# Two more token tiles turned by DMA, x1 on ScalarE's queue, W1 in four parts, no throwaway matmuls between the first transposes, and a new instruction order

## The chip, the cores and the metric

The kernel runs on one core of a Trainium2 chip. The metric is the device time of one execution in microseconds (us); the kernel before takes 150.0 us, the median of three runs (149.98 to 150.35). A core has five instruction streams that run side by side and meet by semaphores: TensorE (PE, matmuls), VectorE (DVE), ScalarE (ACT), GpSimd (POOL) and SyncE (SP). SP computes nothing here; it issues DMAs. ACT and POOL can issue DMAs too.

## The reference

One input x of 2048 tokens by 640 features, in bf16, is normalised, and two branches of the result are added to x:

```
xn  = (x - mean(x)) / sqrt(var(x) + 1e-5)                 # over the 640 features
A   = irfft2( rfft2(xn) * (w_r + 1j * w_i) )               # over tokens and features, in bf16 out
B   = gelu_tanh( xn @ w1 + b1 ) @ w2 + b2                  # 640 -> 1536 -> 640
out = x + A + B
```

The weights are w_r and w_i (2048 x 321), w1 (640 x 1536), b1, w2 (1536 x 640) and b2.

## The kernel before

**Tiles.** The 2048 tokens are 16 tiles of 128 (tile c holds the tokens 16p + c, p the partition). Per tile, DVE takes statistics in two halves (`bn_stats`, L661) and joins them (`bn_aggr`, L663), POOL raises the variance to the power -0.5 (L665), and DVE normalises (L683). The normalised tile goes two ways.

- For branch B it is needed turned, as xnT (features on partitions). Tiles 0 to 5 are turned on PE: five 128x128 transposes against the identity (L702) into PSUM and a copy out of it by DVE or ACT (L557/L558; for tiles 0 and 1 three blocks by DVE and two by ACT). Tiles 6 to 15 (`BYDMA`) are turned by one DMA transpose each, issued on SP (L690).
- For branch A, DVE folds pairs of tiles (L714, L718), and PE begins the transform with ten matmuls for a pair against a table `gtab` ("aps"). Later stages go by the names bps, cps, the filter on DVE (L819, L823), dps, DMA transposes of U (L844), and eps.

**Branch B.** `BLOCKS` groups the tiles as 0, 1, 2-3, 4-5, 6-7, 8-11, 12-15. For each block and each of 12 column blocks of W1, five matmuls (issued as a step of three and a step of two, "hps") fill a PSUM bank, and ACT applies gelu (L752). A group of block 4-5 can't begin before both its tiles are turned. W1 is loaded in three parts, `W1P`: column blocks 0-2 (480 KB), 3-6 (640 KB) and 7-11 (800 KB); a group waits for the part that holds its columns. The second matmul ("kps" for tiles kept early, "fps" for the others) and the last transform step are summed in PSUM, DVE adds x + b2 (L930) and SP stores the tile (L933).

**Order.** Every operation has a number, in the order in which the program builds them, and `ORDER` lists for each of the five engines the numbers in the order of issue. An engine works strictly down its list and waits where an operand is not ready; nothing is reordered while the kernel runs. So a wait in one stream delays all that stands behind it there. `Sched.schedule()` only uses its planned times to choose PSUM banks and buffers; the lists are fixed.

**The start**, as the lists have it:

- SP: x0, x1, W1 part 0, W1 part 1, x2-3, W1 part 2, gtab, x4-5, x6-7, then m, x14-15, e, a part of W2, and so on.
- ACT: b1, the table load for gelu, the identity, then copies and gelu.
- PE: 38 throwaway matmuls on a zeroed tile (`idle(WARM[0], ...)`), two transposes of tile 0, 6 more throwaway matmuls (`idle(WARM[1], ...)`), the little transpose of b1, three transposes of tile 0, five of tile 1, then the groups of blocks 0 and 1.
- DVE: statistics of tile 0, statistics of tile 1, normalise 0, join 1, normalise 1, the copy of three turned blocks of tile 0.

The calls of L541 are loads by the helper `load`; nearly all matmuls are recorded at the helper's line L546, and all copies at L557 (ACT) and L558 (DVE).

Of the kernel before, what the change touches and what calls it, by code (L numbers as in the profile page):

```python
# [9 lines left out]
ACT = mybir.ActivationFunctionType  # L10
# [114 lines left out]
class Pool:  # L125
# [31 lines left out]


ORDER = {
    "sp": """8 12 13 14 15 16 17 18 19 32 28 31 23 33 46 27 47 24 20 25 37 43 164 166 29 48 177 179 190 192 40 41  # L160
34 49 38 42 205 217 219 203 39 30 26 35 36 45 44 521 522 548 546 545 547 524 523 50 569 570 571 572 51 596 595 593
594 622 613 658 649 639 685 675 694 757 748 766 731 711 782 721 798 791 805""",
    "pe": """7 114 115 52 112 120 118 231 237 238 234 267 232 235 268 270 271 273 274 249 243 244 246 247 285 250 286 276 277 282 283 279
280 240 241 291 292 258 259 297 252 253 261 298 262 134 137 294 128 295 288 129 289 327 321 328 322 324 325 146 145 303 306 309
307 304 333 310 334 149 152 330 318 312 313 331 315 319 316 160 336 337 161 354 363 355 366 367 369 370 364 357 372 358 360 373
339 340 264 361 265 173 342 343 174 378 384 385 387 379 396 397 388 393 405 406 348 394 349 345 375 346 187 186 376 408 351 390
409 352 391 200 199 255 423 441 442 424 414 213 212 438 426 256 415 439 226 227 411 420 486 435 427 412 483 436 450 421 504 451
432 433 501 447 448 429 489 606 430 607 608 525 609 417 418 518 632 456 633 381 528 457 634 382 635 515 642 643 644 495 645 459
492 668 669 539 460 453 542 454 670 552 671 402 549 444 300 301 403 498 445 399 704 400 573 705 678 679 563 680 706 566 707 681
576 714 724 725 726 715 727 716 717 587 741 474 590 480 481 475 742 743 468 744 471 472 616 469 617 465 466 462 463 597 477 478  # L170
623 618 652 653 659 619 620 654 695 611 655 656 688 689 637 732 690 647 691 692 751 683 673 752 760 753 754 767 761 762 729 755
746 763 776 764 709 777 792 778 793 785 779 780 786 719 787 788 789 794 795 796 799 800 801 802 803""",
    "act": """11 9 10 53 116 121 239 233 269 272 236 275 245 248 251 287 278 284 281 242 293 260 299 254 135 296 263 132 130 131 290 326
329 323 147 308 305 311 150 335 153 314 332 320 317 338 162 356 368 371 365 359 341 362 266 374 344 175 386 380 389 398 407 350
347 395 188 410 353 392 201 377 702 425 443 604 214 215 257 440 229 722 416 630 488 413 485 428 422 505 452 437 676 503 434 640
490 431 527 526 712 449 419 519 520 666 529 458 383 516 496 494 541 544 455 461 554 550 404 302 499 446 401 574 686 575 564 567
739 577 578 589 614 592 476 591 482 749 473 650 758 470 467 464 598 479 783 624 660 774 697 696 734 733 769 768""",
    "dve": """0 54 55 56 58 59 111 60 117 113 122 119 123 124 126 63 66 62 65 64 67 125 127 133 136 140 139 138 142 143 144 141
73 69 72 70 74 71 79 77 76 148 151 80 154 78 155 81 158 156 159 157 163 165 93 167 90 168 86 83 84 172 87 171
85 88 94 169 95 170 176 91 178 100 92 180 181 189 191 182 101 184 108 102 185 183 98 193 194 97 195 99 196 198 107 197  # L180
202 104 204 109 105 206 207 106 209 211 208 210 218 216 220 221 222 223 225 224 230 228 487 484 506 502 508 512 507 491 511 509
510 514 513 610 530 531 536 532 535 517 537 533 636 497 534 646 538 493 540 543 553 672 551 556 560 500 559 555 557 558 561 562
565 568 708 682 580 584 579 583 582 585 581 728 586 718 588 745 599 600 601 602 603 625 626 627 629 661 628 621 612 662 657 663
664 665 638 648 699 698 693 701 700 684 674 736 735 737 738 770 771 756 747 765 730 773 772 710 781 720 790 797 804""",
    "pool": """2 3 1 57 61 68 22 75 21 4 6 82 89 5 96 103 110 605 703 723 677 631 667 641 713 740 687 651 750 615 784 759
775""",
}


# [17 lines left out]

ROW_NS = {256: 26, 384: 22, 512: 27, 640: 33, 642: 70, 768: 37, 1024: 47, 1280: 56, 1600: 68, 2560: 103, 4096: 160, 10272: 750, "acc": 152}
TAIL = 0.9
LAG = ((1.6, 1.1), (3.9, 2.8), (16.0, 1.6), (60.0, 0.0))  # L210


LAT = {"pe": 0.2, "dve": 0.125, "act": 0.16, "pool": 0.12}
# [2 lines left out]
class Sched:  # L216
# [38 lines left out]
    def schedule(self):  # L255
# [31 lines left out]
        while left:  # L287
            best = None
            for e in self.engines:
                cands = []  # L290
                for o in [p for p in pend[e] if p is fixed[e][len(self.order[e])]] if fixed and len(self.order[e]) < len(fixed[e]) else pend[e]:
# [17 lines left out]
                    t = max(r, free[e])  # L309
# [11 lines left out]
                t, o = min(near, key=lambda c: (-c[1].prio, c[1].seq))  # L321
# [4 lines left out]
            t, e, o = best  # L326
# [8 lines left out]
            if o.nbytes:  # L335
                n, size = o.rows
                ring = rings[e]
                free[e] = ring.issue_end(t, dur, n)
                turn = size == 256 and n == 40
                done = max(t + ring.lead, free[e] - dur + ring.lead, dma_last if turn else dma_free) + n * ROW_NS[size] / 1e3  # L340
                dma_last = max(dma_last, done + lag(t, size))
                if e == "act":
                    done = t + ring.lead + 0.5
                    dma_free += n * ROW_NS[size] / 1e3
                else:
                    dma_free = done
                ring.held.append((done, n))
                o.end = done + TAIL + lag(t, size)
            else:
                o.end = t + dur + LAT[e]  # L350
            for b in o.writes:
# [92 lines left out]


BLOCKS = [(0, 1), (1, 1), (2, 2), (4, 2), (6, 2), (8, 4), (12, 4)]
W1P = [(0, 3), (3, 7), (7, 12)]
GROUPS = [(0, 2), (2, 3), (5, 3), (8, 3), (11, 3), (14, 2)]
BYDMA = tuple(range(6, 16))
ANY = [(0, 8)]  # L450
ZONE = {"hps": [(4, 8)], "bps": [(0, 4)], "cps": [(0, 4)], "dps": [(0, 4)],
        "eps": [(0, 4)], "fin": [(4, 8), (0, 4)], "fps": [(4, 8)], "tps": ANY, "aps": ANY}
# [7 lines left out]
GP = (-81.0, 42.0, 4.0, 72.0, -32.0, 6.0, -9.0)  # L460
G1 = 1
WAVE = (0, 3, 0, 0, 2, 0, 0, 4, 0, 2, 0, 2, 4, 2, 2, 3)
WARM = (38, 6)


def bass_parallel_sum__spectral_gfnet__dense_activation_gelu__prompt_kernel(
# [21 lines left out]
    with ExitStack() as es:  # L488
# [104 lines left out]
            a, b = W1P[j]  # L593
            load(view(W1, 128 * a, [[F, 5], [1, 128 * (b - a)]]), w1v[:, :, 128 * a:128 * b], B_w1s[j], (40, 256 * (b - a)), q=q)
        load_x(0, 1)
        K.op([("act", 1.3)], 420, lambda e, _: e.preload_act_table(ACT.Gelu_apprx_tanh), writes=[Buf("table")])
        load(ident[:], const["I"], B_id, (8, 256), q="act", prio=410)
        load(b1t[:], b1v, B_b1, (1, 256), q="act", prio=405)
        load_x(1, 1)
        load_w1(0)  # L600
        load_w1(1)
        load_x(2, 2)
        load_w1(2)
        load(gtab[:], const["G"], B_g, (8, 4096), issue=0.5)
        load_x(4, 2)
        load_x(6, 2)
# [45 lines left out]
        norm_ops, ring_ops, a_ops, TD = [], [], [], {}  # L652
        B_rs = [Buf(f"rstd{c}") for c in range(16)]
        mv_ops, st_op = [], {}
        for c0, n in [(0, 1), (1, 1)] + [(c, 2) for c in range(2, 16, 2)]:
            pr = 100 - c0 / 2
            B_mv, B_r = Buf(f"mv{c0}"), Buf(f"r{c0}")
            for c in range(c0, c0 + n):
                B_st = Buf(f"st{c}")
                for h in range(2):  # L660
                    st_op[c] = K.op([("dve", 0.393)], pr, lambda e, _, c=c, h=h: e.bn_stats(stats[:, c, 6 * h:6 * h + 6], view(X, c * D + H2 * h, [[1, H2]])),  # L661
                         reads=[B_x[c]], writes=[B_st], gate=mv_ops[:1])
                mv_ops.append(K.op([("dve", 0.119)], pr, lambda e, _, c=c: e.bn_aggr(mv[:, c, :], stats[:, c, :]), reads=[B_st, B_eps], writes=[B_mv]))  # L663
            a, b = c0, c0 + n
            K.op([("pool", 0.65)], 500, lambda e, _, a=a, b=b: e.tensor_tensor(out=rstd[:, a:b], in0=mv[:, a:b, 1], in1=mhalf[:, a:b], op=ALU.pow),  # L665
                 reads=[B_mv, B_mh], writes=[B_r] + B_rs[a:b])

        for pair in range(8):
# [10 lines left out]
            for n in range(2):  # L679
# [16 lines left out]
                for j0, j1, engs in ((0, 3, ["dve"]), (3, 5, ["act"])) if c < 2 else ((0, 5, ["dve", "act"]),):  # L696
                    nj = j1 - j0
                    tps = Buf(f"tps{c}", psum, 1, ZONE["tps"])

                    def xt(e, _, n=n, xnv=xnv, tps=tps, j0=j0, j1=j1):  # L700
                        for j in range(j0, j1):
                            ins = e.transpose(psb(tps.slot, [[1, 512]]).bitcast(BF)[:, 128 * j:128 * j + 128], xnv(n, 128 * j, [[1, 128]]), ident[:])  # L702
                        return ins
                    tp = K.op([("pe", nj * mm_us(128))], pr, xt, reads=[B_xn, xn, B_id], writes=[tps], alts=[[("128", nj * mm_us(128))]])
                    if j0 and not c:
                        idle(WARM[1], WARM[1] * 0.07, gate=[tp])
                    us = {"dve": 0.06 + 0.07 * nj, "act": act_us(128 * nj)}
                    o = K.op([(e, us[e]) for e in engs], pr,
                         copy(lambda c=c, j0=j0, j1=j1: xnT[:, c, j0:j1, :],
                              lambda tps=tps, j0=j0, j1=j1: psb(tps.slot, [[1, 512]]).bitcast(BF)[:, 128 * j0:128 * j1].rearrange("p (j t) -> p j t", j=j1 - j0)),  # L710
                         reads=[tps], writes=[B_xnT[c]])
# [261 lines left out]
```

## Time and profile before

| what | value |
|---|---|
| median of three runs | 150.0 us |
| the profiled execution | 149.5 us |
| span in its trace | 147.5 us, so 2.0 us lie around the span |
| PE busy | 142.1 us, 96% of the span |
| DVE, ACT, POOL busy | 106.8, 87.4, 22.4 us |
| granted PE clock | 1.00 over the span |
| DMA | 23.35 MB, mean 158 GB/s |
| first group of branch B starts on PE | 7.20 us |
| last matmul's chain piece ends | 145.07 us |

Times inside the trace count from the start of the span. A row of the chain of waits gives start, duration, and the work on which the end depends; in a merged row of the timeline, "x38" is the number of instructions, and the idle time before the first, if any, stands in brackets with what ended it. Matmuls are pipelined, so a duration of one (219 ns for a 128-column one) is longer than the distance to the next.

### The profile page before, as it was taken

What the parts mean: (1) busy time and instruction counts of PE and PEld (TensorE: products, weight loads), DVE (VectorE), ACT (ScalarE), POOL (GpSimd) and SP (SyncE); (2) the same over time, 40 slices, a digit from 0 to 9 for tenths busy, and PEclk for the clock granted to TensorE, in tenths of its full rate; (3) what the DMA queues carried; (4) which work ended last, traced back from release to release, by engine and by line L of the source; (5) the groups of instructions that cost most, each with busy time, mean ns of one, the idle gap of its engine ahead of it and who ended that gap; (6) DMA issues with size and microseconds to landing.
All of it is one profiled execution on the core that took longest, in us unless ns stands there. A gap on an engine that the chain in (4) does not pass through costs nothing.

```text
span 147.5 us, 4184 instructions
## 1 busy us (share of the span) xinstructions
PE 142.1 (96%) x1753; PEld 93.0 (63%) x1772; DVE 106.8 (72%) x227; ACT 87.4 (59%) x164; POOL 22.4 (15%) x37
## 2 busy tenths in 40 slices
PE   7999999999999999999999999999999999999993
PEld 7799999988555355456545554554456666556572
DVE  2798999999943469369957966882206969899872
ACT  3288999788998985962547774306587354403000
POOL 1301520401100029040000003000044420000000
PEclk9999999999999999999999999999999999999999
DMA  4999999899989907946406695992639947023233
GB/s 119 325 392 385 349 222 125 212 125 185 157 151 284 200 14 177 260 85 155 43 0 60 126 101 142 146 187 79 132 58 221 212 92 221 21 84 122 107 129 127
DMA packets 30890, 23.35 MB, mean 158 GB/s; under 512 B 19224, under 2 KB 27544, under 8 KB 30744
## 3 DMA queue, kind: packets, MB, share of 16 engines
q1 hardware_dynamic: 28336, 17.48, 51.7%
q0 software_dynamic: 2368, 5.57, 17.5%
q8 instruction: 14, 0.23, 0.7%
q10 hardware_dynamic: 168, 0.04, 0.1%
q14 instruction: 4, 0.03, 0.1%
HBM read 13.58 MB, written 2.62 MB: 110 GB/s over the span
## 4 chain that ended last, share of the span: by engine, by line
PE 93%; DVE 2%; issue 2%; DMA 2%
PE ps L546 92%; DMA X<-in_A_x_dram 2%; PE ps L702 1%; DVE stats L661 1%; DVE T L683 0%; DVE xnT L558 0%; DVE W L930 0%; DVE mv L663 0%
## 5 line engine op out<-in xcount | busy, mean ns | idle before, releaser
L546 PE MATMUL ps<-xnT,W 128*128 128x256 bf16 (+2 forms) x420 | 59.0, 288 | 0.2
L546 PE MATMUL ps<-W,gT 128*128 128x128 bf16 (+3 forms) x378 | 55.7, 291 | 1.6 <-issue 0.9
L546 PEld LDWEIGHTS ps<-W,gT 128*128 128x128 bf16 x396 | 30.0, 98 | 24.0 <-issue 2.2
L546 PEld LDWEIGHTS ps<-xnT,W 128*128 128x128 bf16 x420 | 34.3, 98 | 15.4 <-issue 1.7
L752 ACT ACTIVATE gT<-ps,b1col 128x256 bf16<-128x256 f32 (+2 forms) x84 | 38.4, 512 | 8.7 <-PE ps L546 8.0
L661 DVE BATCH_NORM_STATS2 stats<-X 128x6 f32<-128x320 bf16 x32 | 14.2, 476 | 2.4 <-DMA X<-in_A_x_dram 2.4
L557 ACT ACTIVATE Wf<-ps 128x960 bf16<-128x960 f32 (+1 forms) x9 | 7.6, 879 | 13.3 <-PE ps L546 13.3
L915 POOL DMA_DIRECT2D X<-in_A_x_dram x8 | 7.2, 1350 | 44.5 <-DMA XV<-gtab 23.6
L819 DVE TENSOR_TENSOR T<-Y,Wf 128x1288 bf16<-128x1288 bf16 x16 | 12.4, 824 | 1.3 <-DMA Wf<-in_A_w_i_dram 0.9
L915 POOL DMA_DIRECT2D xnT<-in_A_x_dram x8 | 7.1, 1182 | 24.1 <-DMA XV<-gtab 16.3
L557 ACT ACTIVATE U<-ps 128x512 bf16<-128x512 f32 (+1 forms) x12 | 4.6, 439 | 9.7 <-PE ps L546 9.7
L665 POOL TENSOR_TENSOR rstd<-mv,mhalf 128x2 f32<-128x2 f32 (+1 forms) x9 | 6.3, 698 | 25.5 <-DVE mv L663 25.5
L557 ACT ACTIVATE Xb<-ps 128x960 bf16<-128x960 f32 (+1 forms) x6 | 6.8, 1141 | 5.2 <-PE ps L546 5.0
L557 ACT ACTIVATE Y<-ps 128x644 bf16<-128x644 f32 x11 | 7.6, 708 | 3.8 <-PE ps L546 3.7
L557 ACT ACTIVATE XV<-ps 128x1280 bf16<-128x1280 f32 (+3 forms) x11 | 9.5, 895 | 0.0
L558 DVE CAST Y<-ps 128x644 bf16<-128x644 f32 x5 | 4.1, 828 | 7.0 <-PE ps L546 7.0
L558 DVE CAST Xb<-ps 128x960 bf16<-128x960 f32 (+1 forms) x6 | 6.7, 1122 | 3.0 <-PE ps L546 3.0
L718 DVE TENSOR_TENSOR T<-T 128x512 bf16<-128x512 bf16 (+1 forms) x32 | 8.5, 308 | 0.1
L930 DVE TENSOR_TENSOR W<-ps,xnT 128x640 bf16<-128x640 f32 (+2 forms) x10 | 6.7, 686 | 1.9 <-PE ps L546 1.9
L930 DVE TENSOR_TENSOR W<-ps,X 128x640 bf16<-128x640 f32 x8 | 6.5, 817 | 2.0 <-PE ps L546 1.8
L683 DVE TENSOR_SCALAR T<-X,mv,rstd 128x640 bf16<-128x640 bf16 x16 | 6.6, 440 | 1.5 <-POOL rstd L665 1.5
L546 PE MATMUL ps<-getab,XV 32*128 32x160 bf16 (+1 forms) x128 | 7.6, 242 | 0.0
(50 smaller groups left out, 135.9 us busy)
## 6 DMA issues: line engine op xcount, KB each, us to landing
X<-in_A_x_dram POOLq DMA_DIRECT2D x8, 320.0 KB, 4.8
xnT<-in_A_x_dram POOLq DMA_DIRECT2D x8, 320.0 KB, 5.0
W<-in_B_w_dram SPq DMA_DIRECT2D x5, 480.0 KB, 5.5
out_dram<-W SPq DMA_DIRECT2D x15, 160.0 KB, 1.8
X<-in_A_x_dram SPq DMA_DIRECT2D x7, 320.0 KB, 9.9
Wf<-in_A_w_i_dram SPq DMA_DIRECT2D x6, 160.5 KB, 7.3
Wf<-in_A_w_r_dram SPq DMA_DIRECT2D x6, 160.5 KB, 4.8
W<-in_B_w_dram SPq DMA_DIRECT2D x1, 800.0 KB, 8.1
```

The costliest lines, as they stand in the source:

```text
L546: ins = e.matmul(o_, lhsT=lw, rhs=rh, start=st, stop=sp_, skip_group_check=True)
L557: return e.activation(dst(), src(), ACT.Copy, scale=scale)
L558: return e.tensor_copy(dst(), src())
L661: st_op[c] = K.op([("dve", 0.393)], pr, lambda e, _, c=c, h=h: e.bn_stats(stats[:, c, 6 * h:6 * h + 6], view(X, c * D + H2 * h, [[1, H2]]) ...
L665: K.op([("pool", 0.65)], 500, lambda e, _, a=a, b=b: e.tensor_tensor(out=rstd[:, a:b], in0=mv[:, a:b, 1], in1=mhalf[:, a:b], op=ALU.pow), ...
L683: o = K.op([("dve", 0.356)], pr, lambda e, _, c=c, n=n, xnv=xnv: e.tensor_scalar(out=xnv(n, 0, [[1, D]]), in0=view(X, c * D, [[1, D]]), sc ...
L702: ins = e.transpose(psb(tps.slot, [[1, 512]]).bitcast(BF)[:, 128 * j:128 * j + 128], xnv(n, 128 * j, [[1, 128]]), ident[:])
L718: ring_ops.append(K.op([("dve", dve_us(4 * w, 2))], pr, lambda e, _, op=op, x1v=x1v, xfv=xfv, o_=o_, o0=o0, o1=o1, w=w: e.tensor_tensor(ou ...
L752: K.op([("act", act_us(128 * nt, 1))], pr + PRIO["gelu"] + GP[bi], lambda e, _, c0=c0, nt=nt, fc=fc, hps=hps: e.activation(gT[:, fc, 128 * ...
L819: filt_ops.append(K.op([("dve", dve_us(4 * KP, 2))], pr, lambda e, _, k=k, Y=Y, TB=TB, pair=pair: e.tensor_tensor(out=view(TT, TB.slot * 8 ...
L915: xo_ops[c] = K.op([("pool", 0.9)], 51 - c / 20, lambda e, _, c=c, xov=xov: e.dma_start(xov(0, D), xv[:, c, :], accum_op=ALU.add), reads=[ ...
L930: K.op([("dve", dve_us(w))], 95, lambda e, _, os_=os_, fps=fps, o0=o0, w=w, xov=xov, base=base: e.tensor_tensor(out=view(W1, OST + os_.slo ...
```

## The change

- `BYDMA` begins at 4: tiles 4 and 5 are turned by DMA transposes on SP. Their ten PE transposes and their two copies out of PSUM (both on ACT before) go.
- x1 is loaded through ACT's queue, behind b1 and ahead of the identity; the table load comes after the three. On SP, W1 part 0 is the second load.
- W1 comes in four parts: 480, 640, 480 (column blocks 7-9) and 320 KB (10-11). SP's list is now x0, W1 part 0, W1 part 1, x2-3, W1 part 2, gtab, x4-5, x6-7, W1 part 3, x8-9, b2, a part of W2, the transposes of tiles 4 and 5, x10-11, two loads of w_i, the transposes of tiles 6 and 7, and so on.
- The 6 throwaway matmuls go (`WARM = (38, 0)`). PE's list begins: 38 throwaway matmuls, b1's transpose, tile 0's five transposes, tile 1's five, groups.
- The powers of tiles 2 and 3 are taken one by one on POOL.
- All five lists are new. DVE now joins tile 1's statistics before it normalises tile 0. Of the copies out of PSUM some have passed from ACT to DVE and the other way: tile 3's turned copy and some of Y, U, Xb to ACT, two of the "aps" copies and some of Y, U, Xb to DVE.
- In the planner, two numbers that place the planned landing of DMAs change; they reach the kernel only through the choice of banks.

```diff
 ORDER = {
-    "sp": """8 12 13 14 15 16 17 18 19 32 28 31 23 33 46 27 47 24 20 25 37 43 164 166 29 48 177 179 190 192 40 41
+    "sp": """8 13 14 15 16 18 19 20 17 21 28 30 150 152 25 44 48 163 165 26 29 42 178 176 191 189 27 32 46 31 41 38
...
-    "pe": """7 114 115 52 112 120 118 231 237 238 234 267 232 235 268 270 271 273 274 249 243 244 246 247 285 250 286 276 277 282 283 279
+    "pe": """7 53 116 114 119 121 230 233 234 236 231 237 272 273 269 270 266 267 275 276 278 239 279 284 240 281 285 282 245 246 242 243
...
-    "act": """11 9 10 53 116 121 239 233 269 272 236 275 245 248 251 287 278 284 281 242 293 260 299 254 135 296 263 132 130 131 290 326
+    "act": """9 10 11 12 54 117 122 235 232 238 274 271 268 277 280 241 286 283 247 244 289 256 259 136 139 253 292 131 325 295 132 304
...
-LAG = ((1.6, 1.1), (3.9, 2.8), (16.0, 1.6), (60.0, 0.0))
+LAG = ((1.1, 1.1), (3.9, 2.8), (16.0, 1.6), (60.0, 0.0))
...
-                dma_last = max(dma_last, done + lag(t, size))
+                late = 0.0 if e == "act" else lag(t, size)
+                dma_last = max(dma_last, done + late)
...
-                o.end = done + TAIL + lag(t, size)
+                o.end = done + TAIL + late
...
-W1P = [(0, 3), (3, 7), (7, 12)]
+W1P = [(0, 3), (3, 7), (7, 10), (10, 12)]
-BYDMA = tuple(range(6, 16))
+BYDMA = tuple(range(4, 16))
-WARM = (38, 6)
+WARM = (38, 0)
...
         load_x(0, 1)
-        K.op([("act", 1.3)], 420, lambda e, _: e.preload_act_table(ACT.Gelu_apprx_tanh), writes=[Buf("table")])
+        load(b1t[:], b1v, B_b1, (1, 256), q="act", prio=425, issue=0.65)
+        load_x(1, 1, q="act")
         load(ident[:], const["I"], B_id, (8, 256), q="act", prio=410)
-        load(b1t[:], b1v, B_b1, (1, 256), q="act", prio=405)
-        load_x(1, 1)
+        K.op([("act", 1.3)], 405, lambda e, _: e.preload_act_table(ACT.Gelu_apprx_tanh), writes=[Buf("table")])
         load_w1(0)
         load_w1(1)
         load_x(2, 2)
         load_w1(2)
+        load_w1(3)
...
-        for c0, n in [(0, 1), (1, 1)] + [(c, 2) for c in range(2, 16, 2)]:
+        for c0, n in [(c, 1) for c in range(4)] + [(c, 2) for c in range(4, 16, 2)]:
...
-                    if j0 and not c:
-                        idle(WARM[1], WARM[1] * 0.07, gate=[tp])
```

In the new lists 8, 10, 15, 19, 20 and 21 are the loads of x0, x1, x2-3, x4-5, x6-7 and x8-9; 13, 14, 16 and 17 the parts of W1; 18 is gtab; 150 and 152 are the DMA transposes of tiles 4 and 5, 163 and 165 those of 6 and 7; 53 is b1's transpose on PE.

## The prediction

> **What bounds the kernel now.** I read the page first: the span, PE's row of busy slices, and the summary of the chain that ended last.
>
> ```profile
> span 147.5 us, 4184 instructions
> ...
> PE   7999999999999999999999999999999999999993
> ...
> PE 93%; DVE 2%; issue 2%; DMA 2%
> ```
>
> PE is full from the second slice to the last and is 93% of the chain. So an edit is worth what it takes from PE's work, or what it moves PE's first useful matmul, and a late operand costs in full: no idle time exists in which it could hide. Next the chain in order of time, for the start.
>
> ```profile
> 0.74 2.29 DMA X<-in_A_x_dram
> ...
> 3.98 0.22 DVE mv L663
> 4.20 0.74 DVE stats L661 x2
> 4.94 0.41 DVE T L683
> 5.35 0.05 issue
> 5.40 0.40 PE ps L702 x2
> 5.79 0.68 PE ps L546 x7
> 6.47 0.29 PE ps L702 x3
> ...
> 6.78 0.37 DVE xnT L558
> 7.15 0.05 issue
> 7.20 4.33 PE ps L546 x70
> 11.53 0.10 issue
> ...
> 19.24 0.56 PE ps L702 x10
> ```
>
> Useful work starts at 7.20. Ahead of it lie x0's load, DVE, two transposes, 0.68 us of throwaway matmuls with b1's transpose, three more transposes and a copy. The last row is tiles 4 and 5 on PE. Then a table by stage, who issued the existing DMA transposes and how long they took.
>
> ```profile
> 0.00:7.20 7.20, 5.95 (x56) 5.30 (x56) 3.36 (x11) 1.96 (x4) 1.55 (x9) 1.00 0.73 218
> 7.20:13.00 5.80, 5.70 (x95) 5.31 (x96) 4.84 (x16) 4.78 (x17) 0.70 (x1) 1.00 1.06 393
> 13.00:22.00 9.00, 9.00 (x113) 8.34 (x111) 8.98 (x30) 8.81 (x21) 2.95 (x6) 1.00 1.07 305
> 22.50:36.30 13.80, 13.80 (x148) 12.59 (x147) 13.62 (x46) 12.10 (x27) 2.26 (x4) 1.00 1.03 160
> ```
>
> ```profile
> L690 SPq DMA_TRANSPOSE xnT<-T x10: 1201/1280/2519, 21.7 to 41.7; - x10
> ...
> DMA to landing us min/median/max: 2.6/3.9/5.0
> ```
>
> Columns of the table: stretch, its length, busy PE, weight load, DVE, ACT, POOL, granted clock, DMA share, GB/s. DMA is full from 7.2 on, DVE from 13, ACT is at 88% in the last stretch.
>
> **The change, part by part.** The sum is made in the profiled execution: span 147.5, own time 149.5, so 2.0 around it; the median of the runs is 150.0, 0.5 higher, and I add that at the end.
>
> *Tiles 4 and 5 off PE.* Ten transposes leave the chain: -0.56 (row 19.24). Their copies leave ACT (0.75 and 0.77 in the timeline), which PE did not wait for: 0. Bounds: -0.72 (their busy time) to -0.50.
>
> *The two transposes on SP.* SP must wait for DVE's normalised tiles, and x10, loads of w_i, and tiles 6 and 7 queue behind. In DVE's new list, between normalise 3 (ended 12.83 before, 12.2 to 12.8 now) and normalise 4 stand two folds (0.90), four halves of statistics (1.67), two joins (0.34) and three small folds (0.9): normalise 4 is done at 16.4 to 17.0, normalise 5 one us later. SP needs 1.28 per transpose, so the second is issued at about 17.9. The queue ahead of them is 4672 KB, 4.78 MB. The table moves 1.57 MB by 7.2, 2.28 by 13.0, and the rest at 305 GB/s by about 16.1, so they find little ahead of them. Landing 2.6 to 5.0 later: 20.5 to 22.9; with the median 21.8. PE began block 4-5 at 22.92 before. Ahead of it now stand one more group for tile 0 and one for tile 1 (0.56), ten transposes less (0.56), so it moves with the start alone, to 22.5. Cost 0, bounds 0 to 0.4 by the transposes' own rows; loads issued at 11.7 to 12.8 took 9.9 to 11.7, and by that far row the wait would be 6. I take 0 as the queue is empty by then. Tiles 6 and 7 are wanted about one us earlier than before (at 27.7; landed then by 26.9): 0.
>
> *The start.* Normalise 0 now stands behind tile 1's join, and a join holds DVE 0.14 to 0.22: normalise 0 ends at 5.5. Then b1's transpose is already done, and five transposes follow with nothing between; at the distance of the throwaways (38 in 4.24 us, so 0.106 each) they end by 6.3. Tile 1's join comes 0.31 earlier, so does its power on POOL (0.56), and normalise 1 leaves DVE free at 6.2. The copy (0.37) ends at 6.7 and the first group starts at 6.75 instead of 7.20: -0.45. Bounds: +0.2 (the join alone counts, if something else holds the copy) and -0.6.
>
> *x1 on ACT's queue.* ACT issues it behind b1 (0.62), at about 1.4. DVE wants it at 4.1. The nearest rows: x0 and x1 landed 2.3 and 2.4 after issue, the identity on ACT's own queue 2.3 after 1.42. So 3.8: cost 0. Far row: the 480 KB part took 4.7, which would be 6.1 and delay the whole start by 2.0. The table load (1.28) now ends near 3.6, b1's column is wanted at 7: 0.
>
> *W1 behind x0, four parts.* Part 1 landed at 8.4, and PE wants it after six groups (1.7) at 8.45: 0. Part 2 landed at 11.5 (3.41 + 8.1); 320 KB less at 393 GB/s is 0.8 sooner, and SP is 0.46 earlier without x1: 10.2 to 10.7 against a need at 10.4. gtab (3.88 + 8.9) likewise 11.5 to 12.0 against 11.8. Tile 2 must be normalised by 11.5; with its own join and power it takes some 0.6 less than the 2.75 between x2's landing (2.71 + 6.6) and 12.03, so 11.4 to 11.9. Together 0 to 0.8; I take 0.2, and the 0.1 at 11.53 goes: +0.1.
>
> The Trainium skill (Trainium Kernel Development and Optimization, Key Constraints) says that SP's, ACT's and POOL's DMAs share the same 16 engines, so that a second issuer only saves issue time. By it x1's bytes still stand beside W1's, the later ends hold, and this item would be about 0.5 rather than 0.1; no row here shows x1 there.
>
> *The new order elsewhere.* Same matmuls in another sequence: 0. Final steps end on the same three pieces of tile 15, last store 1.6 after issue: 0. Bounds in the rivals.
>
> Sum: -0.56 - 0.45 + 0.1 = -0.9. Span 146.6, own time 148.6; on the median's scale **149.1**.
>
> **Rivals.** *ScalarE full.* From 22.5 to 36 ACT's new list holds 21 gelus (0.42, the 23 rows' 9.7 us), one small one (0.4), two copies of 1.24 and four copies of b2 (0.75) that stood behind 38 before: 14.7 us, against 13.8 of PE. Back to back five gelus took 1.84, 0.37 each, which makes 13.5. DVE, 13.62 of 13.80, gets one of ACT's copies as well. So PE waits for banks or folds 0 to 0.9; with the upper end 149.9, no change. For: both sums are near 100%. Against: ACT idled 1.7 there and PE never waited.
>
> *PE's clock stays slow.* The timeline has 38 throwaways at 0.106 from 0.99; the 128-column groups from 7.20 run at 95 in 5.99, 0.063. The speed changes inside the six throwaways that go, after some 5.2 us of nearly unbroken work. If the longer break (5.1 to 5.6, then two short ones) starts that stretch anew, it ends at 10.8, and the 4.0 us from 6.75 are done at half speed: 2.0, less the 0.3 that loads would make PE wait anyway. 150.8, slower. It decides from the point at which the change of speed comes later than about 8.5. Against: before, 0.4 without a matmul did not prevent it, and transposes also fill the stretch (eight at 6.40 took 0.71).
>
> The Trainium skill (TensorE: Matmul & The Clock Gate, Part 1 and Part 4) has a free-running window of 3.4 us after which a busy array is released, and says that transposes don't engage the full clock. By it a missed window ends 3.4 later and costs 1.4: 150.5. The trace agrees that both speeds exist, and shows transposes at the fast one; whether they count as work it can't show.
>
> *Turned tiles late.* Landing at 23.8 instead of 21.8 (the slowest row, 5.0, and 0.9 more if the queue ahead isn't empty) stops PE at block 4-5 for 1.3: 150.4. For: PE has no slack. Against: the transpose issued at 24.26, with an empty queue, took 2.6. It decides from 22.5 on.
>
> *x1 late.* From 4.1 on each us is a us; with the far row 151.1.
>
> **Chances.** Forecast 0.50 (148.6 to 149.6 by the bounds of the start and the loads), ScalarE full 0.16, turned tiles late 0.13, clock 0.10, x1 late 0.06, another wait of over one us from the new lists 0.05. About 0.3%, 0.45 us, can be told from no change: faster below 149.55. The forecast gives 0.50 and a mild case of ScalarE 0.04 to faster; the rest of ScalarE, and half a us of lateness in the tiles, 0.18 to the same; slower 0.28. The range runs from the best ends of the bounds (-0.72, -0.6, -0.1: 148.6, less 0.1 for scatter) to the slow clock; the far ends are left out: 148.5 to 150.8.
>
> **What would show it.** Right: in the chain, ten transposes at 19 gone, the first 70-matmul piece at 6.7 to 6.8, PE busy without a gap at 22.5, last piece ending near 144.2. Wrong: normalise 0 waiting for x1; 128-column matmuls 0.106 apart after 6.8; PE idle before the first 256-column group of block 4-5 with a DMA of L690 as releaser; ACT without idle time from 22 to 36 and PE's weight loads released by gelu.

## The result and the profile after

The changed kernel took 151.66 us (median; 150.70 to 152.40) against 149.99 us: a ratio of 1.0123 (95% interval 1.0083 to 1.0163). Forecast were 149.1 us and a gain; 151.66 lies above the range. The profiled execution took 152.04 us.

The page after, answering to the three lines of before:

```profile
span 150.1 us, 4173 instructions
...
PE   7499999999999999999999999999999999999993
...
PE 93%; DMA 4%; ACTq 1%; DVE 0%; issue 0%
```

PE is full to the end as before. Only the second slice (3.75 to 7.5 us) differs: a 4 where a 9 stood. The chain's DVE share has gone, and 4% of DMA has come. The chain in order of time (start, duration, what) says which DMA:

```profile
1.40 0.37 ACTq L542
...
1.80 5.62 DMA ident<-c_I
7.42 0.05 issue
7.47 0.19 PE ps L547
7.65 1.18 PE ps L704 x10
8.83 6.87 PE ps L547 x83
...
16.59 131.10 PE ps L547 x1561
```

The identity, issued at 1.80 behind x1 on ACT's queue, lands at 7.42; before, it landed at 3.75. b1's transpose stands at the head of PE's list and needs it, so PE idles from 5.2 to 7.47. The first group starts at 8.75 by the timeline (7.20 before, 6.75 forecast). From there nothing stops PE: one piece of 1561 matmuls runs from 16.59 to 147.69, and the row of tiles 4 and 5 at 19.24 is gone. So what was lost was lost ahead of 16.6. The 83 matmuls from 8.83 carry the second loss, which an experiment below sizes.

The identity ended the last wait, but x1 was close behind it. DVE's rows in the timeline:

```profile
5.59 0.89 DVE L663 BATCH_NORM_STATS2 stats<-X 128x6 f32<-128x320 bf16 x2 [1.31 <-DMA X<-in_A_x_dram]
6.65 0.38 DVE L685 TENSOR_SCALAR T<-X,mv,rstd 128x640 bf16<-128x640 bf16 x1
7.49 0.45 DVE L685 TENSOR_SCALAR T<-X,mv,rstd 128x640 bf16<-128x640 bf16 x1 [0.46 <-POOL rstd L667]
```

DVE's new list joins tile 1's statistics before it normalises tile 0, so normalise 0 (6.65) waited for x1 too, although its power was there at 4.94; this is a sign of being wrong that the prediction named. Normalise 1 ended at 7.94, and tile 1's transposes stand ahead of the first group. With the identity on time tile 1's transposes could have begun at 7.99 and the first group, by an estimate, at about 8.5 (in the run below with the identity ahead of x1, at half speed too, it started 0.51 behind the first of them: 9.40 and 9.91). So most of the 2.0 us is x1's, and the identity adds 0.2 to 0.3.

The loads issued in the first 2.2 us (the last number is the time from issue to landing):

```profile
X<-in_A_x_dram SPq DMA_DIRECT2D x1, 160.0 KB, 2.4
X<-in_A_x_dram ACTq DMA_DIRECT2D x1, 160.0 KB, 4.2
ident<-c_I ACTq DMA_DIRECT2D x1, 32.0 KB, 5.6
```

x1 took 4.2 on ACT's queue and landed at 5.57, where the forecast had 3.8. The 32 KB of the identity took longer than the 160 KB of x1.

### The profile page after: what moved, and what is told of

Read it like the earlier page. It is cut to its first block, busy times and chain, and to the rows that moved or that the text cites. A ratio compares the mean times of both kernels' runs of the same rounds, so it can differ in the third digit from the quotient of the medians.

```text
span 150.1 us, 4173 instructions
## 1 busy us (share of the span) xinstructions
PE 144.4 (96%) x1756; PEld 94.3 (63%) x1756; DVE 106.8 (71%) x227; ACT 87.4 (58%) x162; POOL 22.9 (15%) x38
## 3 DMA queue, kind: packets, MB, share of 16 engines
q0 software_dynamic: 2368, 5.57, 17.0%
## 4 chain that ended last, share of the span: by engine, by line
PE 93%; DMA 4%; ACTq 1%; DVE 0%; issue 0%
PE ps L547 92%; DMA ident<-c_I 4%; PE ps L704 1%; ACTq L542 1%; DVE W L930 0%
## 5 line engine op out<-in xcount | busy, mean ns | idle before, releaser
L547 PE MATMUL ps<-xnT,W 128*128 128x256 bf16 (+2 forms) x420 | 59.1, 297 | 0.0
L547 PE MATMUL ps<-W,gT 128*128 128x128 bf16 (+3 forms) x396 | 58.5, 295 | 0.0
L547 PEld LDWEIGHTS ps<-xnT,W 128*128 128x128 bf16 x420 | 36.6, 103 | 15.2 <-issue 1.7
L547 PEld LDWEIGHTS ps<-W,gT 128*128 128x128 bf16 x396 | 30.1, 98 | 23.9 <-issue 1.9
L558 ACT ACTIVATE Wf<-ps 128x960 bf16<-128x960 f32 (+1 forms) x8 | 7.0, 902 | 17.8 <-PE ps L547 17.8
L558 ACT ACTIVATE Xb<-ps 128x960 bf16<-128x960 f32 (+1 forms) x8 | 8.7, 1125 | 5.8 <-PE ps L547 5.8
L559 DVE CAST Wf<-ps 128x640 bf16<-128x640 f32 (+1 forms) x4 | 4.0, 989 | 10.5 <-PE ps L547 10.4
L558 ACT ACTIVATE Y<-ps 128x644 bf16<-128x644 f32 x13 | 8.8, 710 | 4.0 <-PE ps L547 4.0
L558 ACT ACTIVATE XV<-ps 128x1280 bf16<-128x1280 f32 (+3 forms) x9 | 8.3, 918 | 0.3 <-PE ps L547 0.3
L921 DVE TENSOR_TENSOR X<-ps,X 128x640 f32<-128x640 f32 x8 | 6.6, 823 | 2.6 <-PE ps L547 2.6
L559 DVE CAST Xb<-ps 128x960 bf16<-128x960 f32 (+1 forms) x4 | 4.6, 1151 | 4.9 <-PE ps L547 4.9
L547 PE MATMUL ps<-getab,XV 32*128 32x160 bf16 (+1 forms) x128 | 7.5, 241 | 0.0
L547 PEld LDWEIGHTS ps<-getab,XV 32*128 32x128 bf16 (+1 forms) x128 | 6.5, 146 | 1.3
```

Source lines behind the costliest of these rows:

```text
L547: ins = e.matmul(o_, lhsT=lw, rhs=rh, start=st, stop=sp_, skip_group_check=True)
L558: return e.activation(dst(), src(), ACT.Copy, scale=scale)
L559: return e.tensor_copy(dst(), src())
L921: kept_ops.append(K.op([("dve", dve_us(D))], 30, lambda e, _, kps=kps, xov=xov: e.tensor_tensor(out=xov(0, D), in0=psb(kps.slot, [[1, D]]) ...
```

## The experiments

**Theory:** the loss is made by x1's place on ACT's queue: x1 and the identity come behind SP's W1 DMAs, and the idle time then keeps PE at half speed for the first groups. **Rivals:** the removed throwaway matmuls alone cost the speed; the turned tiles or the new lists cost something.

### x1 back on SP

```diff
-        load_x(1, 1, q="act")
+        load_x(1, 1)
 SP list:  x0, [x1,] W1 part 0, ...     (x1 taken out of ACT's list)
```

> The changed kernel with one load moved back: x1 on SP behind x0, all else as changed. Theory (the start is lost to x1 and the identity landing late on ACT's queue, and PE's idle time makes its clock slow): x1 lands by 3.7, the identity by 4.2, first group at 6.8, 128-column matmuls 0.056 apart from 8 at the latest, 149.1 us (148.5 to 149.6). Rival A (the six throwaway matmuls held the clock): first group at 6.8 too, but 0.107 apart to 10 or later, 150.3 or more. Rival B (the loss is in the new order or the DMA transposes): over 151.

Measured: 149.06 us, ratio 0.9951 (0.9915 to 0.9987). This one part is the difference between slower and faster. Its chain:

```profile
6.51 0.45 PE ps L706 x5
6.96 0.45 PE ps L549 x8
...
129.90 14.32 PE ps L549 x125
```

The timeline has the first group at 6.80, and the last piece ends at 144.22; the prediction had 6.75 and 144.2. With x1 on SP, the start and the end of the chain came as forecast.

### The identity ahead of x1

```diff
 ACT list: b1, 
-          x1, identity
+          identity, x1
```

> The changed kernel with the identity ahead of x1 on ACT's queue. Theory: the identity lands by 4.2, but x1, issued 0.4 later behind W1, lands at 5.6 to 6.1, so the first group stays at 8.3 to 8.9 and PE still idles for two us: 151.2 to 151.9. Rival (the identity alone holds the start): first group before 7.2, 149.5.

Measured: 152.89 us, ratio 1.0215 (1.0171 to 1.0259): worse than the change, and above the expectation. Its loads:

```profile
X<-in_A_x_dram ACTq DMA_DIRECT2D x1, 160.0 KB, 5.2
ident<-c_I ACTq DMA_DIRECT2D x1, 32.0 KB, 3.6
```

The two changed places, and their times changed with them: the first load of ACT's queue behind W1 takes 3.6 to 4.2, the second 5.2 to 5.6, whether it has 32 or 160 KB. x1 landed at 6.98 (1.80 + 5.18), tile 1 was normalised only after that, and the first group started at 9.91. In between PE stood idle for 3.3 us, and the first 70 matmuls then took 6.26: half speed again.

### W1's first part as two DMAs

```diff
-            load(view(W1, 128 * a, [[F, 5], ...]), w1v[:, :, ...], ..., (40, ...), q=q)
+            for k0, k1 in ((0, 2), (2, 5)) if j == 0 else ((0, 5),):
+                load(view(W1, F * k0 + 128 * a, [[F, k1 - k0], ...]), w1v[:, k0:k1, ...], ..., (8 * (k1 - k0), ...), q=q)
```

This is the changed kernel with part 0 (480 KB) as 192 and 288 KB; x1 and the identity stay on ACT's queue.

> The changed kernel with W1's first part loaded by two DMAs (192 and 288 KB) in place of one, same bytes in the same order; x1 and the identity stay on ACT's queue. Theory (the engines take turns between SP's and ACT's queue, one DMA's worth of descriptors at a time, so the first load on ACT lands with SP's first after x0, the second with SP's second): x1 lands at 4.3 to 4.7 in place of 5.6, the identity at 5.4 to 5.9 in place of 7.4, first group at 7.2 to 7.6; 149.5 with the clock in time, 150.8 without. Rival (the queues share by bytes, or ACT's loads just wait for all of W1's first 1120 KB): x1 at 5.6, the identity at 7.4, 151.7.

Measured: 150.31 us, ratio 1.0009 (0.9970 to 1.0049), less than the change itself; the two intervals don't overlap. Loads issued from 1.3 to 1.9 us:

```profile
W<-in_B_w_dram SPq DMA_DIRECT2D x1, 288.0 KB, 4.1
...
X<-in_A_x_dram ACTq DMA_DIRECT2D x1, 160.0 KB, 3.3
ident<-c_I ACTq DMA_DIRECT2D x1, 32.0 KB, 3.5
```

The same bytes in the same queues, and x1 landed 0.9 us earlier (4.65), the identity 2.1 us earlier (1.80 + 3.5 = 5.3). So it isn't the bytes in flight that held them. ACT's k-th load comes about when the k-th DMA behind x0 of SP's queue is through: with part 0 and part 1 in the change, with the two pieces of part 0 here. The queues take turns, and a turn here was about a whole DMA. The median hides that both times of the expectation came: six of the ten runs show a granted clock of 0.987 to 0.989 and took 150.31 to 150.77, the other four show 1.00 and took 148.78 to 150.15. The profiled one is among the four; its first group started at 7.37, at full speed.

### Keeping PE busy while it waits

```diff
-WARM = (38, 0)
+WARM = (78, 0)
```

The changed kernel with 40 more throwaway matmuls ahead of b1's transpose, so that x1 and the identity are as late as in the change, but PE doesn't idle.

> The changed kernel with 78 throwaway matmuls in place of 38, so that PE works until the identity lands; loads as changed. Theory: the first group stays at 8.7 to 8.9, but its matmuls are 0.056 apart, which takes 2.2 us off: 149.5 (149.1 to 150.0). Rival (the slow matmuls come from something else than the idle time, such as operands): 151.6.

Measured: 149.95 us, ratio 1.0025 (1.0004 to 1.0046), by the ratios 1.5 us less than the change. Its chain:

```profile
0.99 6.73 PE ps L549 x79
...
8.56 4.83 PE ps L549 x83
```

This row stands against `8.83 6.87 PE ps L547 x83` of the change: the same 83 matmuls in 4.83 instead of 6.87, so 2.04 us of the loss is half speed after the idle time. The first group is nearly as late as in the change (8.56 against 8.75). The last piece ends at 145.36 against 147.69.

### x1 on ACT's queue, in the kernel before

```diff
-        load_x(1, 1)
+        load_x(1, 1, q="act")
 ACT list: b1, 
-          table, identity
+          x1, identity, table
```

> The kernel before with x1 and nothing else moved: on ACT's queue behind b1, ahead of the identity and the table load, as in the changed kernel. Theory: x1 lands near 5.6, the identity near 7.4, first group near 8.8, slow matmuls to about 13: 150.0 + 1.6 + 2.2 less 0.3 of waits for W1, 153.4 (152.5 to 154). Rival (x1's queue does not matter; the new order does): 150.0.

Measured: 152.14 us, ratio 1.0138 (1.0073 to 1.0202). The part alone makes the kernel before slower by as much as the whole change does. It missed the expectation on the low side, and the profiled run (150.65) shows why it may: the identity landed at 7.06 and the first group started at 8.64, as in the change, but the 95 matmuls behind it took 5.73 us, 0.060 each: full speed in spite of 1.97 us without work. The other three runs took 151.72 to 153.22. Two of them (152.55 and 153.22) show a granted clock of 0.989 over the run, as two of the change's four do; no run of the kernel before, of x1 on SP or of the 78 throwaways shows less than 0.998. So in one run at least the lateness came without the half speed, in two the clock did fall, and for the run of 151.72 the record doesn't say.

### The six throwaways

```diff
-                        idle(WARM[1], WARM[1] * 0.07, gate=[tp])
+                        pass
```

> The kernel before without its six throwaway matmuls between the first transposes, all else as before. Theory (the six cost 0.4 of the start and hold no clock that the 38 don't already bring): three transposes of tile 0 follow at once, first group at 6.8 to 7.0, W1's second part makes PE wait 0.2 of that; 149.4 where before stands at 149.7 (149.1 to 149.8), with single runs up to 1.5 higher if the change of speed comes late. Rival (they hold the clock): 128-column matmuls 0.107 apart to 9.5 or later in the profile, median over 150.3.

Measured: 151.12 us, ratio 1.0094 (1.0061 to 1.0128), but this run says nothing on the speed. In its profile the matmuls were at full speed from the first group on, which came at 7.00. The loss lies later, in waits on ACT (0.24 at 11.5, 0.25 at 16.4, and more): without the group in the list, `schedule()` plans other times and can choose other PSUM banks, which I take for the cause; no run shows it by itself. So it was done again with one throwaway in place of the six, at the same planned cost, so that the plan stays:

```diff
-                        idle(WARM[1], WARM[1] * 0.07, gate=[tp])
+                        idle(1, WARM[1] * 0.07, gate=[tp])
```

> The kernel before with one throwaway product in place of the six between the transposes of the first two tiles, in the same place of the list and at the same planned cost, so that nothing else of the order moves (taking the group out altogether had moved later waits too). Theory: the six are not what holds the clock, so taking five away gives back 5 x 0.056 = 0.28 us at the start at most: first group 6.9 to 7.2 (7.20 in the kernel before), and part of this is lost again to the wait for W1's third part near 11.4. No slow products after the start. 149.7 us (149.3 to 150.0), ratio 0.995 to 1.000. Rival: the six hold the clock: slow products (0.107 us apart) after the first group, 150.3 us or more, ratio 1.002 or more.

Measured: 149.99 us, ratio 1.0016 (0.9989 to 1.0042): neither a gain nor the loss that the rival asked for is shown. In the profiled run (150.38) the first 95 matmuls from 7.13 took 6.97 us, so here the full speed came late, near 10, as the rival has it; but that is one of twelve runs, and the median is below the rival's 150.3. PE doesn't wait for ACT in it. Whether the six shift the full speed on average isn't settled; what they are worth is below 0.5% by the interval. The best version put such throwaways in again, with x1 on SP:

```diff
-        load_x(1, 1, q="act")        -WARM = (38, 0)
+        load_x(1, 1)                 +WARM = (42, 6)     (the six between the transposes of tile 0 and tile 1)
```

> The version with x1 on SP, with 42 throwaway matmuls at the head and 6 between the transposes of tile 0 and tile 1, which fill the 0.4 us that PE idles in each place. Theory: first group stays at 6.8 to 6.9, and the scatter of the runs (148.3 to 150.9) closes from above, since no run has slow matmuls after the start: median 148.7 (148.3 to 149.1). Rival (the scatter has nothing to do with PE's idle time): the same median and scatter as with x1 on SP, or 0.1 more.

Measured: 149.02 us, ratio 0.9945 (0.9927 to 0.9963). It beats both kernels; against x1 on SP alone (0.9951) the intervals overlap. Its last piece ends at 144.22, too. Five of its six runs lie between 148.84 and 149.12, but the sixth took 151.24, so it isn't shown that the scatter from above is gone. In its profile PE waits 0.21 at 10.99 for W1's part 2 (landed at 10.86): the forecast's wait for the loads.

### Tiles 4 and 5, both ways

First back on PE, in the kernel with x1 on SP:

```diff
-BYDMA = tuple(range(4, 16))
+BYDMA = tuple(range(6, 16))      (PE and ACT lists: after the groups where the kernel before has them)
```

> The version with x1 on SP, and tiles 4 and 5 turned on PE again (ten transposes behind a group of block 2-3, two copies on ACT). Theory: PE's ten transposes come back in full, 0.56 on the version with x1 on SP: PE's last matmul ends at 144.8 in place of 144.2, 149.6. Rival (the DMA transposes gained nothing, since their traffic or SP's waits cost as much): the same as the version with x1 on SP, 149.1.

Measured: 150.75 us, ratio 1.0061 (1.0035 to 1.0087): the sign is as expected, the size three times that. In the chain:

```profile
20.11 0.56 PE ps L706 x10
...
21.94 1.19 ACT xnT L560 x2
```

The ten transposes cost the 0.56 of the sum. The rest includes a wait of 0.40 at 22.0 behind the two copies, as I had put them where ACT was full; this is my place for them, not the change's. PE also waits 0.2 for W1's part 2 (landed at 11.06), and near the end DVE waits 0.78 for a store. How much of the size each makes is not shown.

Then by DMA in the kernel before, with nothing else of the change:

```diff
-BYDMA = tuple(range(6, 16))
+BYDMA = tuple(range(4, 16))
 SP list:  ..., x10, x8, x12, two loads of w_i, 
+          turn tile 4, turn tile 5,
           turn tile 6, ...
```

> One part of the change alone: the kernel before with tiles 4 and 5 turned by DMA; their ten transposes leave TensorE's list, their two copies ScalarE's, and the two DMAs stand ahead of tile 6's in SyncE's queue. All loads at the start are as before. Theory: ten transposes at 0.056 us leave TensorE's chain, nothing waits for the turned tiles (first product of tile 4 at 22.9 in the kernel before, DMAs landing near 22): last product 0.56 us earlier, 149.4 us (149.2 to 149.7), ratio 0.994 to 0.998. Rival: the turned tiles come late, or tiles 6 and 7 behind them do: a wait near 22 to 26 of 0.5 us or more takes the gain, 150.0 us, ratio 1.000 or more.

Measured: 156.65 us, ratio 1.0468 (1.0427 to 1.0508). Both theories missed, the rival's direction held. PE's waits (total, times, longest), the DMAs issued from 18 to 20 us, and the table by stage (stretch, length, busy PE, granted clock, DMA share, GB/s):

```profile
PE ps L548 <- DMA xnT<-T: 5.0, 1, 5.0
```

```profile
xnT<-T SPq DMA_TRANSPOSE x2, 8.0
```

```profile
22.00:28.00 6.00, 0.98 (x11) 0.86 1.30 130
28.00:30.00 2.00, 2.00 (x11) 0.50 1.07 335
30.00:32.00 2.00, 2.00 (x12) 0.50 1.18 178
32.00:34.00 2.00, 2.00 (x15) 0.70 0.76 149
34.00:36.00 2.00, 2.00 (x27) 1.00 0.60 133
```

The turned tiles landed 8.0 us after issue, behind loads that were issued up to 14.6 and landed up to 25.1 in SP's queue. PE stood still for 5.0 us, and then ran at a granted clock of 0.50 for some 5.5 us, which costs half of that, 2.7. 5.0 + 2.7 - 0.56 = 7.1; the ratio makes 7.0 of 149.56. In the changed kernel the same two DMAs:

```profile
xnT<-T SPq DMA_TRANSPOSE x2, 2.9
```

There SP's new list has only 12 loads ahead of them (22 in the other kernel), the last issued at 8.3 and landed at 18.2; the other loads stand behind. So turning two more tiles by DMA gains only together with the new order of SP's list.

## Why the prediction was wrong, by its steps

**The step that failed** is "x1 on ACT's queue": "So 3.8: cost 0". Its nearest row, "the identity on ACT's own queue 2.3 after 1.42", was a load issued ahead of SP's W1 (1.42 against 1.66). In the change W1 is issued at 1.21, and x1 at 1.40 stands behind it. The far row (4.7, the 480 KB part; 6.1 and +2.0) was nearly what came: 4.2, 5.57. I took the queue's name for the likeness that counts; the order of issue across both queues was.

The Trainium skill has the rule that I didn't weigh (DMA: Bandwidth & Descriptors, Queues, rings and completion order): each of the 16 engines goes round the queues that have work, and drains a packet of descriptors of one before it turns to the next. The runs agree in kind: loads with 160 and with 32 KB changed places and kept the times of the places. The Trainium skill calls 9 to 17 descriptors typical for a packet and gives 64 as the ceiling. Here a turn lasted about as long as a whole DMA of W1.

**What the prediction didn't see:** the identity, moved behind x1 in the same queue, comes one turn later still (7.42), and b1's transpose at the head of PE's list, which needs it, holds all of PE's list. Only x1 was costed. The identity alone adds little here (0.2 to 0.3 by the estimate above), but it is what PE waited for.

**The rivals "x1 late" and "clock stays slow"** both came, at 0.06 and 0.10, each priced alone (151.1 and 150.8). "x1 late" was right in its mechanism. "Clock stays slow" was right in its effect and not in its cause: it put it down to the throwaways that go, but with x1 on SP, and the six still gone, the transposes from 5.61 were 0.06 apart, at full speed. Here the late operands make the idle time that keeps the clock down (without it, with 78 throwaways, the speed was full). Together the two are the result. That the price of the slow clock agrees, 2.0 forecast and 2.04 measured, is in part luck: it was made for the 4.0 us from 6.75, and half speed lasted some 4.5 us from 8.75.

The account from the forecast end (144.2) to the measured one (147.69), +3.5: first group 8.75 instead of 6.75, +2.0; half speed, +2.04; from the first group to the end 138.94 - 2.04 = 136.9 instead of 144.2 - 6.75 = 137.45, -0.55. Most of this -0.55 lies in the first 83 matmuls: with x1 on SP they took 5.28 (6.80 to 12.08), with pauses of some 0.2 at 7.4, for a copy on ACT, and 0.3 at 10.9, which the chain puts down to a gelu (ended 10.81), but W1's part 2 landed then, too (10.8); with the late start and 78 throwaways they took 4.83.

**What held:**

- *Tiles 4 and 5 off PE*, -0.56: the row of ten is gone, nothing new waits, and 0.56 came back when they were put back.
- *The two transposes on SP*, 0 "as the queue is empty by then": 2.9 from issue to landing, no wait. As the change started 2.0 late, the fairer test is x1 on SP: 2.7 and 4.3 from issue to landing, PE busy for all of 22.5 to 36.3. The queue was empty near 18.0 there, not by 16.1 as forecast, and the second tile landed at 22.31, less than half a us before block 4-5 began (22.76): the sum was right, with little to spare. The far row ("the wait would be 6") came true at 5.0 where the queue wasn't empty.
- *The start*, 6.75: 6.80 with x1 on SP.
- *W1 in four parts*: part 1 landed at 7.84 and part 2 at 10.17, no wait in the change, whose start was late. With the start on time part 2 landed at 10.8 to 10.9, later than the 10.2 to 10.7 of the sum, and PE paused 0.2 to 0.3 there, near the 0.2 that the sum took.
- *ScalarE full* did not come: from 22.5 to 36.3 ACT was busy 12.78 of 13.80 us in the change and 12.77 with x1 on SP, and PE all of it in both. *Turned tiles late* did not come either, for the reason that the last experiment shows.

## What to carry to other kernels

In these runs a load's landing time couldn't be read from rows of its own queue or of its size, but from what was issued ahead of it in both queues. So put what the first useful work needs ahead of the large loads, on either queue, with some margin (issued at 1.42 against W1's 1.66, the identity took 2.3 in the kernel before, but 3.4 without the six throwaways and 2.9 with tiles 4 and 5 turned by DMA there), and count everything that moves with it. Where late operands leave a matmul engine idle, price the clock in the same case, not as a rival beside it. A DMA that a full queue would delay can be added only with an order of that queue that leaves it empty by then.

## What the runs showed of the hardware

- The time from the start of nearly unbroken matmul work to full speed: 5.8 us in the change (7.47 to 13.3), about 5.2 before, about 5.5 after the wait with tiles 4 and 5 turned by DMA in the kernel before. In some it was shorter: with 42 and six throwaways full speed came at 4.25, 3.3 after the first. I had worked with one window of 3.4 as the price by the Trainium skill (TensorE: Matmul & The Clock Gate, Part 1). But the Trainium skill calls that window free-running, so that work which starts inside one must fill the next: by an estimate from that, 3.4 to 6.8 after the start. The traces named so far agree with that reading (3.3 to 5.8); as an estimate it would have given 1.7 to 3.4 as the price, against 2.04 measured. One profile doesn't fit: with one throwaway in place of the six, full speed came only at 10.1, 9.1 after the first matmul. PE paused there up to 0.2 at a time between 5.2 and 6.6, as it also did in the kernel before; why it came so late stays open.
- The granted clock of the table isn't enough by itself: in the change it reads 1.00 from 1.0 to 17, although 83 matmuls took 6.87 instead of 4.83 there. With tiles 4 and 5 turned by DMA in the kernel before, where the speed fell in the middle of the run, it reads 0.50. Matmuls for each us show the speed in both.
- How long the idle time may be isn't one number here: after 1.97 us the speed was full (x1 on ACT's queue in the kernel before, the profiled run), after 2.24 in the change half. After 3.30 with the identity ahead of x1 it was half until 14.5, although the speed had been full at 4.26 already.
